# State kept zero-padded, and output products run together with the next chunk's state update

## The chip, the cores and the metric

The kernel runs on one core of one Trainium2 chip. Times are device microseconds (us) of one execution. The profile shows the engines of that core: PE (TensorE, matrix products; its weight loads are listed apart, as PEld), DVE (VectorE), ACT (ScalarE), POOL (GpSimd) and SP (SyncE, which here only starts transfers).

## The reference

Two parts follow each other. The first is linear attention with a state of its own for each of 4 batches and 8 heads (768 tokens, head width 48, all float32):

```
for t in range(S):
    cur = einsum('bhd,bhe->bhde', u * kt, vt)
    y[:, :, t] = einsum('bhd,bhde->bhe', rt, state + cur)
    state = wt[:, :, :, None] * state + einsum('bhd,bhe->bhde', kt, vt)
```

The second is a feed-forward block over the 3072 tokens (width 384, hidden width 2048): `h = x @ w_in`, `g = h * sigmoid(1.702 h)`, `out = g @ w_out`.

## The kernel before, in words

**The feed-forward part.** Tokens are taken in six groups of 512 (`CHUNKS`, four chunks of 128 each), the hidden width in 16 slices of 128. One task is a group and a slice. A task has a first product (token `g`, lines 346 to 348: nine matmuls of 128x128 weights with 512 columns), the gelu (token `h`, lines 357 to 359: two passes on ACT, one on DVE) and a second product (token `y`, lines 372 to 374: nine matmuls). Each product is made of three, from high and low halves of the numbers. `y` runs two tasks behind `g` (`LAG`). There are 106 tasks; group 0 is cut finer at its start.

**The attention part.** There are 24 chunks of 128 tokens, six to a batch. A chunk needs the state that the chunk before it left; a batch's first chunk has none, and its last leaves none. The eight heads are four pairs: a pair's two heads lie on partitions 0 to 47 and 64 to 111 (`head(h)`). `chunk(t)` is a generator of twelve pieces, which the text counts from 0:

- pieces 0 to 2 (DVE): two scans of the decays, products with k and r, which give `kf` and `qf` (lines 224 to 246);
- piece 3: `ps_d` matmuls (line 252), in chunks 0 to 7 only;
- piece 4 (DVE): diagonal sums `s`, and the old state times the chunk's total decay, in place (line 262);
- piece 5: `kf` transposed on PE (line 268) and copied to `kt` by ACT (line 270);
- piece 6 (ACT): eight diagonal matrices `am` (line 277);
- piece 7: the state update: `ps_u` = `kt` times `v` (lines 284 and 285, 16 matmul records), added to the decayed state by DVE (line 290; ACT copies it where there is no old state, line 288);
- piece 8: score matmuls `ps_s` (line 296); piece 9: they are copied into `am` by a mask (DVE, line 299);
- piece 10: the outputs, `ps_y`: `am` times `v` (line 309, 16 matmul records), then, on the same accumulators, the state product, old state times `qf` (line 316, 16 matmul records);
- piece 11: `ps_y` is split into high and low halves of the feed-forward input `x` (ACT line 194, DVE line 195).

A float32 product appears in the records as two matmuls, so 16 records are 8 products: four pairs, two heads. Line 309 and the state update use all 128 partitions as rows and 64 or 48 columns of the array. Line 316 uses 48 rows and 48 columns: head 0's state is at rows and columns 0 to 47, head 1's at 64 to 111.

All small PSUM tiles share three buffers (`psa`). `kt`, `lp` and each of the two `am` tiles have one buffer, `kq` and the state two.

**Order of the work.** It is written out by hand. The first part is the list `RAMP`, up to task 41, which also loads and converts the weights (tokens `f` and `w`: 12 conversions on ACT and DVE, lines 180 to 190). From task 42 (`FIRST`) on, `rest()` makes the order from `PARTS`: a list of pieces with the step at which each comes, counted from the chunk's begin, either ahead of the task's `g` (0) or behind it (1). Tokens `l` load a chunk, `m` measures it (ACT, line 200), `x` starts the DMAs (line 334) that fill the gaps of `x`. In this order, every four tasks, one chunk puts four groups of small matmuls between the big ones, each behind another `g`: `ps_t`, then `ps_u`, then `ps_s`, then `ps_y`.

Of the kernel before, what the change touches and what calls it, by code (L numbers as in the profile page):

```python
# [8 lines left out]
F32 = mybir.dt.float32  # L9
# [4 lines left out]
AF = mybir.ActivationFunctionType  # L14
# [38 lines left out]
TASKS += [(0, 2, 4, f) for f in range(5, 10)] + [(0, 0, 4, f) for f in range(10, NF)]  # L53
TASKS += [(i, 0, n, f) for i, n in enumerate(CHUNKS) if i for f in range(NF)]

PARTS = [("a", 0, 0), ("a", 1, 0), ("a", 2, 0), ("m", 2, 0), ("a", 2, 1), ("a", 3, 0), ("m", 3, 0), ("l", 3, 0),
         ("l", 3, 0), ("a", 3, 1), ("a", 4, 0), ("a", 4, 1), ("a", 5, 1), ("a", 5, 1), ("a", 6, 1), ("a", 6, 1), ("x", 6, 1)]
BEFORE = 9

# [14 lines left out]
y38 a13 y39 h40 x11 g41 h41 m12  # L76
"""
WIDE = 512
PAD = 528
assert sum(CHUNKS) == NT  # L80


# [1 line left out]
def rwkv_ffn_kernel(ctx: ExitStack, tc, wkr, vp, vrk, ub, w_in, w_out, masks, vt, uc, out):  # L84
# [41 lines left out]
    acc = cp.tile([P, 2 * NT + 2 * NL], F32, name="acc")  # L126
    G.memset(acc, 0.0)
    wih, wil, woh, wol = (cp.tile([P, NF, DM], F32R, name=x) for x in ("wih", "wil", "woh", "wol"))

    loaded, state, pools = {}, {}, {}  # L130

# [79 lines left out]
    def chunk(t):  # L211

        i, col = where[t]
        a, v = loaded[t][:2]
        n, nc_ = NP * CW, NP * C
        w0, w1 = a[:, 0:n], a[:, 1 : n + 1]
        k = a[:, n + 1 : n + 1 + nc_].rearrange("r (p c) -> r p c", p=NP)
        r = a[:, n + 1 + nc_ :].rearrange("r (p c) -> r p c", p=NP)
        first, final = t % CB == 0, (t + 1) % CB == 0

        lp = at.tile([R2, 2 * n], F32, tag="lp", name="lp")
        li, pm = (lp[:, i * n : (i + 1) * n].rearrange("r (p c) -> r p c", p=NP) for i in range(2))
        total = li[:, :, 0:1]
        V.tensor_tensor_scan(  # L224
            li.rearrange("r p c -> r (p c)")[:, ::-1], w1[:, ::-1],
            d1r.rearrange("r p c -> r (p c)")[:, ::-1], 0.0, op0=ALU.mult, op1=ALU.add,
        )
        V.reciprocal(d1f[:, :, 0:1], total)
        yield
        V.tensor_tensor_scan(  # L230
            pm.rearrange("r p c -> r (p c)"), w0,
            d1f.rearrange("r p c -> r (p c)"), 0.0, op0=ALU.mult, op1=ALU.add,
        )
        s = at.tile([P, H], F32, tag="s", name="s", bufs=2)
        if t < WHOLE:
            rk = at.tile([R2, NP, C], F32, tag="rku", name="rku")
            V.tensor_tensor(rk, r, k, op=ALU.mult)
        else:
            rt, kt_ = loaded[t][2][:, 0:DM], loaded[t][2][:, DM:]
            V.tensor_tensor(rt, rt, kt_, op=ALU.mult)  # L240
        yield

        kq = at.tile([R2, 2 * nc_], F32, tag="kq", name="kq", bufs=2)
        kf, qf = (kq[:, i * nc_ : (i + 1) * nc_].rearrange("r (p c) -> r p c", p=NP) for i in range(2))
        V.tensor_tensor(kf, k, li[:, :, 1:CW], op=ALU.mult)
        V.tensor_tensor(qf, r, pm[:, :, 0:C], op=ALU.mult)
        measures[t] = measured(t, lp, kq)
        yield
        if t < WHOLE:
            ps_d = ps_a.tile([P, NP, 2], F32, tag="psa", name="ps_d")  # L250
            for p in range(NP):
                T.matmul(ps_d[:, p], rk[:, p], u_heads[:, p], start=True, stop=True)  # L252
        yield
        if t < WHOLE:
            V.tensor_copy(s, ps_d.rearrange("p n h -> p (n h)"))
        else:
            V.tensor_tensor(rt, rt, u_sb, op=ALU.mult)
            V.tensor_reduce(s, rt.rearrange("p (h d) -> p h d", d=D), axis=AX.X, op=ALU.add)
        sf = None
        if not first:  # L260
            sf = state[t - 1]
            V.tensor_tensor(sf, sf, total.broadcast_to([R2, NP, D]), op=ALU.mult)
        loaded.pop(t)
        yield
        if not final:
            ps_t = ps_a.tile([P, NP, R2], F32, tag="psa", name="ps_t")
            for p in range(NP):
                T.transpose(ps_t[:, p], kf[:, p], ident[0:R2, 0:R2])  # L268
            kt = at.tile([P, NP, R2], F32, tag="t", name="kt")
            A.copy(kt, ps_t)  # L270
        yield
        am = []
        for h in range(2):
            x_ = at.tile([P, NP, C], F32, tag=f"am{h}", name="am")
            am.append(x_)
            for p in range(NP):
                A.activation(x_[:, p], ident, AF.Copy, scale=s[:, 2 * p + h : 2 * p + h + 1])  # L277
        yield

        if not final:  # L280
            ps_u = ps_a.tile([R2, NP, D], F32, tag="psa", name="ps_u")
            for p in range(NP):

                T.matmul(ps_u[0:HB, p], kt[:, p, 0:HB], v[:, 2 * p], start=True, stop=True)  # L284
                T.matmul(ps_u[HB:R2, p], kt[:, p, HB:R2], v[:, 2 * p + 1], start=True, stop=True)  # L285
            new = state[t] = at.tile([R2, NP, D], F32, tag="sf", name="sf", bufs=2)
            if sf is None:
                A.copy(new, ps_u)
            else:
                V.tensor_tensor(new, ps_u, sf, op=ALU.add)  # L290
        yield

        ps = [ps_a.tile([P, NP, C], F32, tag="psa", name=f"ps_s{h}") for h in range(2)]
        for p in range(NP):
            for h in range(2):
                T.matmul(ps[h][:, p], kf[head(h), p], qf[head(h), p], start=True, stop=True)  # L296
        yield
        for h in range(2):
            V.copy_predicated(am[h], after_b, ps[h])  # L299
        yield  # L300
        cs = slice(col * C, (col + 1) * C)
        ps = ps_a.tile([R2, NP, C], F32, tag="psa", name="ps_y")
        v_ = v.rearrange("p h d -> p (h d)")

        for p in range(NP):
            for h in range(2):
                at_, m = ((0, HB), (HB, D))[h]
                c = (2 * p + h) * D
                T.matmul(  # L309
                    ps[at_ : at_ + m, p], v_[:, c : c + m], am[h][:, p],  # L310
                    start=p == 0, stop=sf is None and p == NP - 1, skip_group_check=True,
                )
        if sf is not None:
            for p in range(NP):
                for h in range(2):
                    T.matmul(  # L316
                        ps[head(h), p], sf[head(h), p], qf[head(h), p],
                        start=False, stop=p == NP - 1, skip_group_check=True,
                    )
        yield  # L320
        if i not in xs:
            xs[i] = new_x(i)
        x = xs[i]
        split(x[0:R2, 0, :, cs], x[0:R2, 1, :, cs], ps)
        state.pop(t - 1, None)
        yield
# [8 lines left out]
                    x[dst : dst + 16, :, m, c0:c1].bitcast(F32), x[j : j + 16, :, NM, c0:c1].bitcast(F32)  # L335
                )

    xs, po, parts, measures = {}, {}, {}, {}

    def first_product(j, task):  # L340
        i, c0, c1, f = task
# [46 lines left out]
    with tc.manual_schedule():  # L388
# [17 lines left out]
        def do(token):  # L406
# [18 lines left out]
            elif kind == "u":  # L425
                nc.sync.dma_start(u_sb, ub)
            elif kind == "M":
                A.dma_start(hm[0:D], masks[0:D])
                A.dma_start(hm[HB:R2], masks[D:R])
            elif kind == "g":  # L430
                first_product(i, TASKS[i])
            elif kind == "h":
                gelu(i, TASKS[i])
            elif kind == "y":
                second_product(i, TASKS[i])
                group = TASKS[i][0]
                if i == last[group]:
                    store(group, starts[group] * C, CHUNKS[group] * C)

        def rest():  # L440

            begins = []
            for t, (i, col) in enumerate(where):
                n = len([x for x in TASKS if x[0] == i - 1])
                begins.append(last.get(i - 1, -1) + 1 - BEFORE - round((CHUNKS[i] - 1 - col) * n / CHUNKS[i]))
            ramp = dict(told)
            for j in range(FIRST, len(TASKS) + LAG):
                for post in range(2):
                    if post and j < len(TASKS):
                        yield f"g{j}"  # L450
                        yield f"h{j}"
                    for t, begin in enumerate(begins):
                        for kind, step, half in PARTS:
                            token = f"{kind}{t + 2 * (kind == 'l')}"
                            if (step + begin, half) > (j, post) or kind == "l" and t + 2 >= NT:
                                continue
                            if ramp.get(token, 0):
                                ramp[token] -= 1
                            elif (step + begin, half) == (j, post):
                                yield token  # L460
                if j - LAG >= 0 and f"y{j - LAG}" not in told:
                    yield f"y{j - LAG}"

        for token in RAMP.split():
            do(token)
        for token in rest():
            do(token)

# [116 lines left out]
```

## Time and profile before

| What | Value |
|---|---|
| Time, median of 3 runs | 549.38 us (547.93 to 551.22) |
| The profiled execution | 545.92 us, of which 544.3 us lie between its first and last instruction |
| Granted TensorE clock, mean | 0.994 of full |
| PE busy | 521.7 us (96%), 3462 matmul records |
| DVE busy, ACT busy | 282.4 us (52%), 284.0 us (52%) |

A row of the page's groups has a line, an engine and operation, the tile written and those read, shapes, the count, then the busy time in us and the mean time of one in ns, then the idle time ahead of them on that engine. A row of the timeline has the start in us, the time from the first start to the last end of the instructions merged in it, the engine and line, and the count. Matmuls overlap in the array, so that what a matmul costs is the distance to the next one's start and not its own length.

### The profile page before, as it was taken

To read this page: it belongs to the slowest core of one execution; us is meant where nothing else is said; L and a number is where in the kernel's file an instruction comes from. 1 tells how busy PE (TensorE), PEld (TensorE's weight loads), DVE (VectorE), ACT (ScalarE), POOL (GpSimd) and SP (SyncE) were. 2 spreads that over 40 slices of the span, in tenths; PEclk is the share of its full clock that TensorE was granted. 3 is DMA by queue.
4 is the path that set the end of the run, shared out by engine and by line. 5 is a ranking of instruction groups with operands and counts; after the bars stand their busy time and mean duration, and the time that the engine had idled before them with its cause. 6 is when DMAs were issued, how large, how long until landed. Compare 5 with 4: busy or idle time off the path is not lost.

```text
span 544.3 us, 8703 instructions
## 1 busy us (share of the span) xinstructions
PE 521.7 (96%) x3462; PEld 431.8 (79%) x3462; DVE 282.4 (52%) x438; ACT 284.0 (52%) x616; POOL 32.4 (6%) x69
## 2 busy tenths in 40 slices
PE   2898999999999999999999999999999999999994
PEld 1788999888878788787777787788788787888883
DVE  4798798977635563553544554545445423112110
ACT  2888868976635545655354364454364442322221
POOL 3110200000100001000001000001000001000000
PEclk9999999999999999999999999999999999999998
DMA  8989899243623432234313244213240001010001
GB/s 190 212 170 220 194 225 230 58 97 95 182 51 95 96 97 70 67 88 94 66 30 91 56 131 94 54 43 83 63 133 1 0 1 31 21 39 0 1 0 64
DMA packets 17506, 48.10 MB, mean 88 GB/s; under 512 B 3024, under 2 KB 6416, under 8 KB 17456
## 3 DMA queue, kind: packets, MB, share of 16 engines
q1 hardware_dynamic: 14096, 36.02, 26.0%
q0 software_dynamic: 3104, 11.13, 10.1%
q8 instruction: 29, 0.48, 0.4%
q10 hardware_dynamic: 256, 0.30, 0.2%
q14 instruction: 21, 0.17, 0.1%
HBM read 40.36 MB, written 4.72 MB: 83 GB/s over the span
## 4 chain that ended last, share of the span: by engine, by line
PE 89%; DMA 2%; DVE 1%; ACT 1%; SPq 0%; issue 0%
PE po L372 14%; PE ph L346 12%; PE po L374 12%; PE po L373 12%; PE ph L348 12%; PE ph L347 12%; PE ps_s L296 4%; PE ps_y L309 4%; PE ps_y L316 3%; DMA st<-in_w_out 2%; PE ps_u L284 1%; PE ps_t L268 1%; PE ps_d L252 1%; PE ps_u L285 1%; SPq L334 0%; DVE st L183 0%
## 5 line engine op out<-in xcount | busy, mean ns | idle before, releaser
L359 DVE TENSOR_TENSOR gl<-gf,gh 128x512 fp32r<-128x512 f32 (+1 forms) x106 | 67.6, 639 | 204.9 <-ACT gf L358 201.6
L357 ACT ACTIVATE gh<-ph 128x512 fp32r<-128x512 f32 (+1 forms) x106 | 59.0, 557 | 184.6 <-PE ph L348 176.4
L372 PE MATMUL po<-gh,woh 128*128 128x512 f32 (+1 forms) x318 | 123.5, 388 | 0.0
L346 PE MATMUL ph<-x,wih 128*128 128x512 f32 (+1 forms) x318 | 120.3, 378 | 0.0
L348 PE MATMUL ph<-x,wil 128*128 128x512 f32 (+1 forms) x318 | 118.7, 373 | 1.4 <-DVE wil L190 1.4
L347 PE MATMUL ph<-x,wih 128*128 128x512 f32 (+1 forms) x318 | 118.6, 373 | 0.0
L374 PE MATMUL po<-gl,woh 128*128 128x512 f32 (+1 forms) x318 | 118.4, 372 | 0.0
L373 PE MATMUL po<-gh,wol 128*128 128x512 f32 (+1 forms) x318 | 118.3, 372 | 0.0
L372 PEld LDWEIGHTS po<-gh,woh 128*128 128x128 f32 x318 | 60.7, 191 | 13.6 <-issue 2.6
L348 PEld LDWEIGHTS ph<-x,wil 128*128 128x128 f32 x318 | 61.1, 192 | 11.8 <-DVE wil L190 1.6
L346 PEld LDWEIGHTS ph<-x,wih 128*128 128x128 f32 x318 | 61.1, 192 | 11.2 <-issue 1.0
L374 PEld LDWEIGHTS po<-gl,woh 128*128 128x128 f32 x318 | 60.6, 191 | 10.6 <-DVE gl L359 0.3
L347 PEld LDWEIGHTS ph<-x,wih 128*128 128x128 f32 x318 | 61.2, 192 | 9.7
L373 PEld LDWEIGHTS po<-gh,wol 128*128 128x128 f32 x318 | 60.7, 191 | 8.6
L277 ACT ACTIVATE am<-ident,s 128x128 f32<-128x128 f32 x192 | 58.8, 398 | 7.3 <-PE ps_y L309 5.7
L358 ACT ACTIVATE gf<-ph 128x512 f32<-128x512 f32 (+1 forms) x106 | 58.7, 553 | 0.0
L299 DVE COPY_PREDICATED am<-after,ps_s 128x512 f32<-128x512 int32 x48 | 32.6, 729 | 5.9 <-ACT am L277 3.3
L224 DVE TENSOR_TENSOR_SCAN lp<-wkr_t,d1r 112x516 f32<-112x516 f32 x24 | 29.5, 1229 | 6.2 <-POOL d1r L102 4.2
L296 PE MATMUL ps_s<-kq 48*128 48x128 f32 x384 | 31.8, 304 | 0.0
L296 PEld LDWEIGHTS ps_s<-kq 48*128 48x128 f32 x384 | 26.6, 204 | 5.8 <-issue 4.6
L309 PE MATMUL ps_y<-am,v_t 128*64 128x128 f32 (+1 forms) x384 | 29.2, 291 | 0.5 <-DVE am L299 0.5
L230 DVE TENSOR_TENSOR_SCAN lp<-wkr_t,d1f 112x516 f32<-112x516 f32 x24 | 29.4, 1224 | 0.1
(62 smaller groups left out, 473.9 us busy)
## 6 DMA issues: line engine op xcount, KB each, us to landing
wkr_t<-in_wkr SPq DMA_DIRECT2D x23, 385.2 KB, 5.0
wkr_t<-in_wkr POOLq DMA_DIRECT2D x23, 288.9 KB, 5.5
st<-in_w_out SPq DMA_DIRECT2D x6, 1024.0 KB, 10.4
rk_t<-in_vrk SPq DMA_DIRECT2D x16, 384.0 KB, 4.5
v_t<-in_vrk SPq DMA_DIRECT2D x24, 192.0 KB, 4.5
out_t<-ob SPq DMA_DIRECT2D x18, 256.0 KB, 2.0
st<-in_w_in POOLq DMA_DIRECT2D x6, 384.0 KB, 9.6
st<-in_w_in SPq DMA_DIRECT2D x6, 384.0 KB, 11.4
```

The lines of the kernel that those rows point to most:

```text
L277: A.activation(x_[:, p], ident, AF.Copy, scale=s[:, 2 * p + h : 2 * p + h + 1])
L296: T.matmul(ps[h][:, p], kf[head(h), p], qf[head(h), p], start=True, stop=True)
L309: T.matmul(ps[at_ : at_ + m, p], v_[:, c : c + m], am[h][:, p], start=p == 0, stop=sf is None and p == NP - 1, skip_group_check=True,)
L346: T.matmul(ph, h_, xs[i][:, 0, c, cs], start=c == 0, stop=False)
L347: T.matmul(ph, h_, xs[i][:, 1, c, cs], start=False, stop=False)
L348: T.matmul(ph, l_, xs[i][:, 0, c, cs], start=False, stop=c == NM - 1)
L357: A.activation(gh, ph, AF.Gelu_apprx_sigmoid, scale=1.0 / W_SCALE)
L358: A.activation(gf, ph, AF.Gelu_apprx_sigmoid, scale=1.0 / W_SCALE)
L359: V.tensor_tensor(gl, gf, gh.bitcast(F32), op=ALU.subtract)
L372: T.matmul(o, woh[:, f, ms], gh, start=first, stop=False, skip_group_check=True)
L373: T.matmul(o, wol[:, f, ms], gh, start=False, stop=False, skip_group_check=True)
L374: T.matmul(o, woh[:, f, ms], gl, start=False, stop=f == NF - 1, skip_group_check=True)
```

## The change

Each chunk's state is kept in a tile of twice the width: a pair's two heads have a column block each, and the rows that belong to the other head hold zeros. Two such tiles are filled with zeros by POOL in the ramp, and the chunks take them in turn. So the state product of line 316 takes all 112 partitions as rows (with `qf` of both heads as the moving data) and 48 columns, that is, the array's rows are no longer divided there. The decay multiplies the wide tile; the add of the state update, and the copy where there is no old state, is done once for each head. The state update takes 48 columns for both heads.

From task 42 on (`steady`), pieces 6 and 7 change places: the update comes first and the diagonals second. `PARTS` puts the outputs of a chunk (its last two pieces) and the update and diagonals of the next chunk behind the same task's `g`, the outputs first; `BEFORE` goes from 9 to 11, so that a chunk begins two tasks earlier, and its last two pieces stay behind the same task as before. Pieces of chunks 12 and 13 whose place in the new order lies ahead of task 42 are put at its start, half a step apart. In the ramp the order is as it was. The list `tiled` is never filled, so its branch is not run, and the extra `x` tokens for chunks that don't end a group do nothing. The spare tile `PAD` shrinks by what the state tiles grow.

```diff
-PARTS = [..., ("m", 3, 0), ("l", 3, 0),
-         ("l", 3, 0), ("a", 3, 1), ("a", 4, 0), ("a", 4, 1), ("a", 5, 1), ("a", 5, 1), ("a", 6, 1), ("a", 6, 1), ("x", 6, 1)]
-BEFORE = 9
+PARTS = [..., ("m", 3, 0), ("a", 3, 1), ("a", 4, 1),
+         ("a", 4, 1), ("l", 5, 0), ("l", 5, 0), ("a", 5, 1), ("a", 5, 1), ("a", 8, 1), ("a", 8, 1), ("x", 8, 1)]
+BEFORE = 11
...
-PAD = 528
+PAD = 144
...
+    states = [at.tile([R2, NP, 2, D], F32, tag=f"sf{i}", name="sf") for i in range(2)]
...
-            V.tensor_tensor(sf, sf, total.broadcast_to([R2, NP, D]), op=ALU.mult)
+            flat = sf.rearrange("r p h d -> r p (h d)")
+            V.tensor_tensor(flat, flat, total.broadcast_to([R2, NP, R]), op=ALU.mult)
...
+        def update():
...
             for p in range(NP):
-                T.matmul(ps_u[0:HB, p], kt[:, p, 0:HB], v[:, 2 * p], start=True, stop=True)
-                T.matmul(ps_u[HB:R2, p], kt[:, p, HB:R2], v[:, 2 * p + 1], start=True, stop=True)
-            new = state[t] = at.tile([R2, NP, D], F32, tag="sf", name="sf", bufs=2)
-            if sf is None:
-                A.copy(new, ps_u)
-            else:
-                V.tensor_tensor(new, ps_u, sf, op=ALU.add)
+                for h in range(2):
+                    T.matmul(ps_u[head(h), p], kt[:, p, head(h)], v[:, 2 * p + h], start=True, stop=True)
+            new = state[t] = states[t % 2]
+            for h in range(2):
+                if sf is None:
+                    A.copy(new[head(h), :, h], ps_u[head(h)])
+                else:
+                    V.tensor_tensor(new[head(h), :, h], ps_u[head(h)], sf[head(h), :, h], op=ALU.add)
+        for part in (update, diagonal) if steady else (diagonal, update):
+            part()
+            yield
...
                     T.matmul(
-                        ps[head(h), p], sf[head(h), p], qf[head(h), p],
+                        ps[head(h), p], sf[:, p, h], qf[:, p],
                         start=False, stop=p == NP - 1, skip_group_check=True,
                     )
...
+                for sf in states:
+                    G.memset(sf, 0.0)
```

More of the change, by code (lines that the diff above doesn't have):

```diff
@@ L54 @@
 TASKS += [(i, 0, n, f) for i, n in enumerate(CHUNKS) if i for f in range(NF)]
-PARTS = [("a", 0, 0), ("a", 1, 0), ("a", 2, 0), ("m", 2, 0), ("a", 2, 1), ("a", 3, 0), ("m", 3, 0), ("l", 3, 0),
-         ("l", 3, 0), ("a", 3, 1), ("a", 4, 0), ("a", 4, 1), ("a", 5, 1), ("a", 5, 1), ("a", 6, 1), ("a", 6, 1), ("x", 6, 1)]
-BEFORE = 9
+PARTS = [("a", 0, 0), ("a", 1, 0), ("a", 2, 0), ("m", 2, 0), ("a", 2, 1), ("a", 3, 0), ("m", 3, 0), ("a", 3, 1), ("a", 4, 1),
+         ("a", 4, 1), ("l", 5, 0), ("l", 5, 0), ("a", 5, 1), ("a", 5, 1), ("a", 8, 1), ("a", 8, 1), ("x", 8, 1)]
+BEFORE = 11
 FIRST = 42
@@ L265, in chunk @@
         if not final:
-            ps_t = ps_a.tile([P, NP, R2], F32, tag="psa", name="ps_t")
-            for p in range(NP):
-                T.transpose(ps_t[:, p], kf[:, p], ident[0:R2, 0:R2])
             kt = at.tile([P, NP, R2], F32, tag="t", name="kt")
-            A.copy(kt, ps_t)
-        yield
[L272 to L277, printed above, removed]
@@ L278, in chunk @@
-        yield
-        if not final:
+            if tiled:
+                ps = [ps_a.tile([P, NP, D], F32, tag="psa", name=f"ps_t{h}") for h in range(2)]
+                for p in range(NP):
+                    for h in range(2):
+                        T.transpose(ps[h][:, p], kf[head(h), p], ident[head(h), head(h)])
+                for h in range(2):
+                    A.copy(kt[:, :, head(h)], ps[h])
+            else:
+                ps_t = ps_a.tile([P, NP, R2], F32, tag="psa", name="ps_t")
+                for p in range(NP):
+                    T.transpose(ps_t[:, p], kf[:, p], ident[0:R2, 0:R2])
+                A.copy(kt, ps_t)
@@ L281, in chunk, with diagonal @@
+        yield
+        am, sums = [], []
+        def diagonal():
+            for h in range(2):
+                x_ = at.tile([P, NP, C], F32, tag=f"am{h}", name="am")
+                am.append(x_)
+                for p in range(NP):
+                    A.activation(x_[:, p], ident, AF.Copy, scale=s[:, 2 * p + h : 2 * p + h + 1])
+        def update():
+            if final:
+                return
             ps_u = ps_a.tile([R2, NP, D], F32, tag="psa", name="ps_u")
             for p in range(NP):
-                T.matmul(ps_u[0:HB, p], kt[:, p, 0:HB], v[:, 2 * p], start=True, stop=True)
@@ L285, in chunk @@
-                T.matmul(ps_u[HB:R2, p], kt[:, p, HB:R2], v[:, 2 * p + 1], start=True, stop=True)
-            new = state[t] = at.tile([R2, NP, D], F32, tag="sf", name="sf", bufs=2)
-            if sf is None:
-                A.copy(new, ps_u)
-            else:
-                V.tensor_tensor(new, ps_u, sf, op=ALU.add)
-        yield
+                for h in range(2):
+                    T.matmul(ps_u[head(h), p], kt[:, p, head(h)], v[:, 2 * p + h], start=True, stop=True)
+            new = state[t] = states[t % 2]
@@ L293, in chunk @@
+            for h in range(2):
+                if sf is None:
+                    A.copy(new[head(h), :, h], ps_u[head(h)])
+                else:
+                    V.tensor_tensor(new[head(h), :, h], ps_u[head(h)], sf[head(h), :, h], op=ALU.add)
+        for part in (update, diagonal) if steady else (diagonal, update):
+            part()
+            yield
         ps = [ps_a.tile([P, NP, C], F32, tag="psa", name=f"ps_s{h}") for h in range(2)]
@@ L336, in fill_x @@
                 )
-    xs, po, parts, measures = {}, {}, {}, {}
+    xs, po, parts, measures, tiled, steady = {}, {}, {}, {}, [], []
     def first_product(j, task):
@@ L445, in rest @@
                 begins.append(last.get(i - 1, -1) + 1 - BEFORE - round((CHUNKS[i] - 1 - col) * n / CHUNKS[i]))
-            ramp = dict(told)
+            done, plan = dict(told), {}
+            for t, begin in enumerate(begins):
+                late = 0
+                for kind, step, half in PARTS:
+                    token = f"{kind}{t + 2 * (kind == 'l')}"
+                    if done.get(token, 0):
+                        done[token] -= 1
+                    elif kind != "l" or t + 2 < NT:
+                        at_ = 2 * (step + begin) + half
+                        if at_ < 2 * FIRST:
+                            at_ = 2 * FIRST + late
+                            late += 1
+                        plan.setdefault(at_, []).append(token)
             for j in range(FIRST, len(TASKS) + LAG):
@@ L451, in rest @@
                         yield f"h{j}"
[L452 to L460, printed above, removed]
+                    yield from plan.get(2 * j + post, ())
                 if j - LAG >= 0 and f"y{j - LAG}" not in told:
@@ L465, in rwkv_ffn_kernel @@
             do(token)
+        steady.append(True)
         for token in rest():
```

## Prediction

> **What bounds the kernel now.** I read the page first, then the waits of PE, then the timeline of PE around one chunk. From the page:
>
> ```profile
> PE 521.7 (96%) x3462; PEld 431.8 (79%) x3462; DVE 282.4 (52%) x438; ACT 284.0 (52%) x616; POOL 32.4 (6%) x69
> ...
> PE   2898999999999999999999999999999999999994
> ...
> PE 89%; DMA 2%; DVE 1%; ACT 1%; SPq 0%; issue 0%
> ```
>
> PE is busy in all but the first slices, and 89% of the chain that ended last is PE. Among the waits of PE the last one in time that is worth naming is this, and the chain of waits shows what it waited for:
>
> ```profile
> PE ph L348 <- DVE wil L190: 1.4, 1, 1.4
> ```
> ```profile
> 49.30 0.26 DVE sf L262
> 49.57 1.15 DVE wil L190
> ```
>
> So up to 50.7 us the ramp is bound by transfers, ACT and DVE, and an edit there is worth what it does to DVE. Behind that PE never stops, and each microsecond taken out of PE's sequence is a microsecond of the span, as long as no other engine becomes late. What small matmuls cost PE is read from distances between starts. One chunk's outputs and state product, from the timeline of PE:
>
> ```profile
> 329.21 0.39 PE L348 MATMUL ph<-x,wil 128*128 128x512 f32 x1
> 329.53 1.09 PE L309 MATMUL ps_y<-am,v_t 128*64 128x128 f32 x16
> 330.55 1.08 PE L316 MATMUL ps_y<-kq,sf 48*48 48x128 f32 x16
> 331.55 0.50 PE L372 MATMUL po<-gh,woh 128*128 128x512 f32 x1
> 331.89 0.39 PE L373 MATMUL po<-gh,wol 128*128 128x512 f32 x1
> ```
>
> and a stretch of the ramp in which a state update happens to follow an output run directly:
>
> ```profile
> 124.77 0.39 PE L346 MATMUL ph<-x,wih 128*128 128x512 f32 x1
> 125.00 0.39 PE L347 MATMUL ph<-x,wih 128*128 128x512 f32 x1
> 125.22 0.39 PE L348 MATMUL ph<-x,wil 128*128 128x512 f32 x1
> 125.45 0.55 PE L268 MATMUL ps_t<-ident,kq 112*128 112x112 f32 x4
> 125.93 1.09 PE L309 MATMUL ps_y<-am,v_t 128*64 128x128 f32 x16
> ...
> 127.40 0.50 PE L372 MATMUL po<-gh,woh 128*128 128x512 f32 x1
> 127.73 0.40 PE L373 MATMUL po<-gh,wol 128*128 128x512 f32 x1
> ```
>
> Big matmuls start 0.225 us apart (125.22 less 124.77, halved). The run at 329 costs 331.89 - 329.21 - 2 x 0.225 = 2.23 us. Within it the length of one matmul gives the stride (columns: least, median, greatest length in ns):
>
> ```profile
> L309 PE MATMUL ps_y<-am,v_t x384: 272/273/476, 20.8 to 455.2; 128*48 128x128 f32 x168, 128*64 128x128 f32 x24
> ```
>
> The 16 records of line 309 last 1.09 us, the last of them 0.273, so they start (1.09 - 0.273)/15 = 0.054 us apart, the last at 330.35. Line 316 begins 0.20 us later, at 330.55: at the place where the array goes from whole columns to quadrants the distance is 0.20 instead of 0.054.
>
> **State products in whole-row tiles.** Line 316 keeps its 16 records, each with 128 columns streamed. In the new shape they stand on line 309's division of the array (all rows, 48 of 64 columns), so I price them at line 309's stride, and the step between the lines at the same 0.054. That saves 0.20 - 0.054 = 0.15 us a chunk. From below: nothing is saved, if the 0.20 comes from something else than the division. From above: 0.15 is all that there is. I take 0.15, since the merged stretch of the ramp (next part) shows that a change of tile and operands without a change of division is cheap. 20 of the 24 chunks have a state product, 10 of them (13 to 17, 19 to 23) behind the ramp.
>
> The Trainium skill, in "TensorEngine Tiling (Array Packing)", Key Properties, says that different tiles can load and multiply in parallel; by that the old quadrants, two of which are used in turn, would run two heads at once, and the change would give that up, at an estimate of half of 16 x 0.054 us a chunk, 8.6 us over 20 chunks. The trace disagrees: 16 records in quadrants take 1.08 us, 16 that fill all rows take 1.09.
>
> **Update and outputs in one run.** Before, the update stands alone:
>
> ```profile
> 340.03 0.39 PE L348 MATMUL ph<-x,wil 128*128 128x512 f32 x1
> ...
> 341.28 0.39 PE L373 MATMUL po<-gh,wol 128*128 128x512 f32 x1
> ```
>
> It costs 341.28 - 340.03 - 0.45 = 0.80 us. In the ramp stretch above, line 309's last start is 125.93 + 0.82 = 126.75, and the next big matmul comes at 127.40, 0.65 later. With no update between, that distance is 331.55 - (330.55 + 0.81) = 0.19. So the update costs 0.46 us inside a run: saved are 0.34 us. Behind the ramp the updates of chunks 14, 15, 16 and 18 to 22 join a run of the chunk before (chunks 17 and 23 have none): 8 x 0.34 = 2.7 us. From above it would be nine with chunk 13's, from below zero, if the joined update had to wait. It needs `kt`, which ACT copies a whole task earlier; its PSUM buffer comes from the previous chunk's scores, masked three tasks earlier. Neither is near. What is now queued on ACT behind the output's cast is the eight diagonals, a task ahead of the masking that needs them, and then the group's stores; PE has over 4 us of big products meanwhile. If that cover were gone, masking would wait, and with it only `ps_y` three tasks later.
>
> **The seam at task 42.** Here the new order puts chunk 12's outputs, chunk 13's transposes, its `kt` copy and its update behind one `g`. The copy cannot be early: ACT runs gelu, the cast, then the copy. These are ACT's rows at that place, and the copy's mean:
>
> ```profile
> 226.38 0.60 ACT L357 ACTIVATE gh<-ph 128x512 fp32r<-128x512 f32 x1 [3.23 <-PE ph L348]
> 226.88 0.59 ACT L358 ACTIVATE gf<-ph 128x512 f32<-128x512 f32 x1
> 227.42 0.59 ACT L194 CAST x<-ps_y 112x512 fp32r<-112x512 f32 x1
> ```
> ```profile
> L270 ACT COPY kt<-ps_t 128x448 f32<-128x448 f32 x20 | 10.7, 536 | 29.2 <-PE ps_t L268 29.2
> ```
>
> The copy would end near 227.42 + 0.59 + 0.54 = 228.55. PE gets there earlier. Its row for the same outputs:
>
> ```profile
> 226.28 1.09 PE L309 MATMUL ps_y<-am,v_t 128*64 128x128 f32 x16
> ```
>
> The last of them starts at 227.10, then 0.20 for the change and the four transposes (0.48 from their start to the next line's, 125.45 to 125.93): 227.8. PE waits 0.75 us, once, and everything behind it on PE with it. Two more changes of division in that run cost about 0.2, and joining saves 0.34: together +0.6 us. Chunk 13's second scan and products move ahead of task 42 on DVE; they need only what the ramp has loaded, and DVE is half idle there, so I cost this at nothing.
>
> **Added work on DVE, ACT and POOL.** From the groups by line:
>
> ```profile
> L240 DVE TENSOR_TENSOR rk_t<-rk_t 128x384 f32<-128x384 f32 x16 | 8.5, 532 | 0.0
> ...
> L262 DVE TENSOR_TENSOR sf<-sf,lp 112x192 f32<-112x192 f32 x20 | 7.0, 348 | 0.0
> ...
> L290 DVE TENSOR_TENSOR sf<-ps_u,sf 112x192 f32<-112x192 f32 x16 | 5.6, 349 | 4.9 <-PE ps_u L285 4.9
> ```
>
> The wide decay is priced as line 240, which has its 384 elements: +0.18 us, 20 times. The add becomes two of half the partitions; I take each at the full 0.35, so +0.35, 16 times (from below +0). The page's 52% for DVE is an average over stages; for the tight one I take a row of the windows (stretch, its length, then busy time and count of PE, PEld, DVE, ACT and POOL):
>
> ```profile
> 50.70:114.00 63.30, 63.24 (x544) 59.72 (x545) 56.88 (x81) 52.33 (x110) 6.17 (x13) 0.97 0.74 163
> ```
>
> DVE is 90% busy between 50.7 and 114 us, and there two places matter. First, chunk 3's decay lies on the chain at 49.30 just ahead of the `wil` on which PE waits: +0.18, and about 0.1 from chunk 1's doubled add earlier, while chunk 3's state product gives back 0.15. Second, the transposes of chunk 6 at 113.86 follow closely on their operand:
>
> ```profile
> 112.73 0.68 DVE L246 TENSOR_TENSOR kq<-wkr_t,lp 112x512 f32<-112x512 f32 x1
> ```
> ```profile
> 113.86 0.58 PE L268 MATMUL ps_t<-ident,kq 112*128 112x112 f32 x4
> ```
>
> The slack is 113.86 - 113.41 = 0.45; DVE is late by one doubled add and one wide decay, 0.53. So chunk 4's gain is lost there and 0.08 more. Up to 114 us that makes about +0.2. Behind it chunks 5 and 7 to 11 gain 6 x 0.15 = 0.9. POOL's two fills come in the first microseconds, ahead of two weight transfers, and hide in what ACT and DVE then wait for other things.
>
> **The sum.** 10 x 0.15 = 1.5 and 2.7 and 0.9 saved, 0.6 and 0.2 paid: -4.3 us. Against the profiled execution, 545.92 us (544.3 between its instructions), this is 541.6. That execution is 3.5 us below the median of the runs shown; the forecast for the median is 549.38 - 4.3 = 545.1. A change of 0.5%, 2.75 us, is about what a measurement of this kernel can tell from no change.
>
> **Rivals.** (a) *The 0.20 us step stays*, because it belongs to the change from one line's operands to the next and not to the division. Against it: at 126.75 the same kind of step cost at most 0.46 with all 16 records of the update. Then 1.5 + 0.9 are not saved and chunk 3's 0.15 too: about -1.8, 547.6.
>
> (b) *DVE bounds more of the ramp than I read.* All that it gets up to 114 us (five wide decays, four doubled adds, 0.9 + 1.4 = 2.3) reaches PE instead of 0.2: -2.2, 547.2. For it speaks the 90%; against it that DVE idles for ACT and transfers several times within the stretch.
>
> (c) *With all rows taken, the weight load no longer hides.* Both heads' tiles now use the same rows, where quadrants used different ones. The loads last:
>
> ```profile
> L309 PEld LDWEIGHTS ps_y<-am,v_t 128*64 128x64 f32 (+1 forms) x384 | 22.4, 136 | 8.0 <-issue 5.4 <-DVE am L299 1.1 <-DVE kq L245 0.4
> L316 PEld LDWEIGHTS ps_y<-kq,sf 48*48 48x48 f32 x320 | 17.1, 123 | 3.7 <-issue 3.6
> ```
>
> If each of the 320 loads stood in series with the matmul before it, 320 x 0.123 = 39 us would be added: 584. It decides from 4.3/320 = 13 ns per record on (no gain left), and is a loss that can be measured from 22 ns. Against it: line 309's loads last 136 ns on whole rows, and its matmuls still start 54 ns apart. The Trainium skill, in "TensorE: Matmul & The Clock Gate", Part 3, states that a load overlaps running matmuls only where the row group differs; by that rule line 309 would already run at over 136 ns a record, and the trace disagrees.
>
> (d) *The joined update waits in every run* as it does at the seam: 8 x 0.75 = 6 us, +1.7, 551.1. For it I find no queue; it stands for what I overlook.
>
> **Chances.** Forecast 0.70, (a) 0.10, (b) 0.10, (c) 0.04, (d) 0.06. The likeliest case gives 545.1, in it from 543.3 (all 20 products and nine updates gain: -6.1) to 547. Runs of the old kernel lie 1.5 to 1.8 us off their median, so the lower end is 541.8; the upper, which takes in (a) and (b) with that scatter, is 549.2. Faster by over 0.5%: 0.66 (nearly all of the forecast, a little of (a) and (b)); within 0.5%: 0.27; slower: 0.07, (c) and half of (d).
>
> **What would show it.** In the changed profile line 316 should have the shape 112*48 and start 0.05 after line 309's last; a run with outputs, state product and update should cost 2.23 - 0.15 + 0.46 = 2.54 us instead of 2.23 + 0.80; one wait of `ps_u` on `kt` of 0.75 us near task 43, and only one; no new wait of PE on DVE but about 0.1 at chunk 6's transposes. Strides above 60 ns in line 316 would make it (c), a step of 0.20 between the lines (a), and waits of `ps_u` in each run (d).

## The result and the profile after

The changed kernel takes 542.80 us in the median of 4 runs (541.80 to 543.58), against 549.29 us (547.93 to 551.22, 4 runs) before: a ratio of 0.9878, with a 95% interval of 0.9844 to 0.9913. That is 6.5 us less, where 4.3 were forecast. The profiled execution took 543.58 us, 542.0 of them between its instructions, at a granted clock of 0.982.

From the page of the changed kernel, its engines, PE's slices and the summary of the chain:

```profile
PE 512.2 (95%) x3462; PEld 428.9 (79%) x3462; DVE 294.4 (54%) x454; ACT 284.5 (52%) x620; POOL 32.8 (6%) x71
...
PE   1788899999999999999999999999999999999994
...
PE 86%; ACT 3%; DMA 3%; SPq 1%; DVE 1%; issue 0%; ACTq 0%
```

PE has the same 3462 records and is busy 9.5 us less. DVE has 12.0 us more. The chain is still mostly PE, so the question is again where PE's starts lie.

The profile that came with the changed kernel is only 2.3 us below the one of before (543.58 and 545.92), though the medians are 6.5 apart. Two rows show why. The first is the start of the 25th task's first product, just behind the ramp, the second that of the 106th and last. From the timeline of PE before:

```profile
116.40 0.50 PE L346 MATMUL ph<-x,wih 128*128 128x512 f32 x1
...
527.94 0.39 PE L346 MATMUL ph<-x,wih 128*128 128x512 f32 x1
```

and after:

```profile
120.06 0.50 PE L366 MATMUL ph<-x,wih 128*128 128x512 f32 x1
...
526.00 0.39 PE L366 MATMUL ph<-x,wih 128*128 128x512 f32 x1
```

Between them lie 411.54 us before and 405.94 after: 5.60 us saved in PE's sequence. Up to the first of them the changed kernel is 3.66 us later. The experiments show that this start moves by 2 to 3 us between executions whose work up to there is the same. Two things make it late in this profile: PE waits 2.35 us at 67.35 for a transfer that fills `x`, and from 68.6 to 72.0 us the granted clock is 0.50, where big matmuls of 256 columns start 0.21 us apart instead of 0.12. From the 9th to the 11th first product that costs 1.3 us. Between the 25th and the 106th the granted clock is 1.00 in every profile of this study, so the clock has no part in the 5.60.

What became of one chunk's run, now with the next chunk's update in it, stands in the timeline of PE after:

```profile
370.94 0.39 PE L368 MATMUL ph<-x,wil 128*128 128x512 f32 x1
371.26 1.09 PE L329 MATMUL ps_y<-am,v_t 128*64 128x128 f32 x16
372.18 1.04 PE L336 MATMUL ps_y<-kq,sf 112*48 112x128 f32 x16
373.05 0.53 PE L301 MATMUL ps_u<-v_t,kt 128*48 128x48 f32 x16
373.51 0.50 PE L392 MATMUL po<-gh,woh 128*128 128x512 f32 x1
373.85 0.40 PE L393 MATMUL po<-gh,wol 128*128 128x512 f32 x1
```

By the prediction's rule the run costs 373.85 - 370.94 - 0.45 = 2.46 us, where 2.23 + 0.80 = 3.03 were paid before and 2.54 were forecast. The last record of line 329 starts at 371.26 + 1.09 - 0.27 = 372.08, and line 336 begins 0.10 later; before, that step was 0.20.

The timeline merges the 16 records of a line. Taken singly from the trace, they start two by two: one record for head 0's half of the columns and one for head 1's, 0.007 us apart, and the next two 0.109 later. Before, the quadrants of line 316 do the same. So 0.054 is a mean that no two records keep, and a step of 0.10 between two lines is no more than the distance within a line: at the entry to the state product nothing extra is left. Before, two things were extra there: 0.10 at the entry, and 0.03 behind the first two records of line 316 (0.147 to the next two, against 0.113 in line 336).

At the seam (behind the first product of task 43, with tasks counted from 0 as in the code), from the same view:

```profile
228.42 0.39 PE L368 MATMUL ph<-x,wil 128*128 128x512 f32 x1
228.74 1.09 PE L329 MATMUL ps_y<-am,v_t 128*64 128x128 f32 x16
229.76 0.60 PE L280 MATMUL ps_t<-ident,kq 112*128 112x112 f32 x4
230.98 0.56 PE L301 MATMUL ps_u<-v_t,kt 128*48 128x48 f32 x16 [0.62 <-ACT kt L281]
231.48 0.50 PE L392 MATMUL po<-gh,woh 128*128 128x512 f32 x1
231.81 0.39 PE L393 MATMUL po<-gh,wol 128*128 128x512 f32 x1
```

The forecast wait of `ps_u` on `kt` is there. The bracket counts 0.62 us from the end of the last transpose; by the prediction's working, from where the update could have started, it is 230.98 - 229.76 - 0.48 = 0.74. The run costs 2.94 us. Its three parts stood apart before, at 1.22, 0.41 and 0.80, so the seam costs 0.51 us net. Behind the 25th first product it is the only wait of PE on another engine.

The groups by line of the changed kernel show the state product, its loads, the add and the decay:

```profile
L336 PE MATMUL ps_y<-kq,sf 112*48 112x128 f32 x320 | 22.2, 281 | 0.0
L336 PEld LDWEIGHTS ps_y<-kq,sf 112*48 112x48 f32 x320 | 19.4, 129 | 0.0
...
L307 DVE TENSOR_TENSOR sf<-ps_u,sf 48x192 f32<-48x192 f32 x32 | 11.2, 350 | 4.4 <-PE ps_u L301 4.2
L265 DVE TENSOR_TENSOR sf<-sf,lp 112x384 f32<-112x384 f32 x20 | 11.0, 548 | 0.0
```

The doubled add takes 350 ns each time, and the wide decay 548 instead of 348: +0.35 and +0.20 a chunk, as forecast (+0.35 and +0.18). The loads of line 336 last 129 ns instead of 123, and its 16 records start (1.04 - 0.27)/15 = 0.051 us apart on average.

### The profile page after: what moved, and what is told of

It is laid out like the page before. It is cut to its first block, busy times and chain, and to the rows that moved or that the text cites. A ratio compares the mean times of both kernels' runs of the same rounds, so it can differ in the third digit from the quotient of the medians.

```text
span 542.0 us, 8721 instructions
## 1 busy us (share of the span) xinstructions
PE 512.2 (95%) x3462; PEld 428.9 (79%) x3462; DVE 294.4 (54%) x454; ACT 284.5 (52%) x620; POOL 32.8 (6%) x71
## 4 chain that ended last, share of the span: by engine, by line
PE 86%; ACT 3%; DMA 3%; SPq 1%; DVE 1%; issue 0%; ACTq 0%
PE po L392 13%; PE ph L366 12%; PE po L394 12%; PE po L393 12%; PE ph L368 12%; PE ph L367 12%; PE ps_s L316 4%; PE ps_y L329 4%; PE ps_y L336 3%; DMA st<-in_w_out 2%; PE ps_u L301 1%; PE ps_t L280 1%; DMA x<-x 1%; PE ps_d L254 1%; SPq L354 1%; ACT am L291 0%
## 5 line engine op out<-in xcount | busy, mean ns | idle before, releaser
L368 PE MATMUL ph<-x,wil 128*128 128x512 f32 (+1 forms) x318 | 118.5, 372 | 1.3 <-DVE wil L192 1.3
L394 PE MATMUL po<-gl,woh 128*128 128x512 f32 (+1 forms) x318 | 118.4, 372 | 0.0
L329 PEld LDWEIGHTS ps_y<-am,v_t 128*64 128x64 f32 (+1 forms) x384 | 22.9, 139 | 9.1 <-issue 5.5
```

The costliest lines, as they stand in the source:

```text
L329: T.matmul(ps[at_ : at_ + m, p], v_[:, c : c + m], am[h][:, p], start=p == 0, stop=sf is None and p == NP - 1, skip_group_check=True,)
L368: T.matmul(ph, l_, xs[i][:, 0, c, cs], start=False, stop=c == NM - 1)
L394: T.matmul(o, woh[:, f, ms], gl, start=False, stop=f == NF - 1, skip_group_check=True)
```

## The experiments

Three theories were to be told apart. *The division*: what is saved is the array's change from whole rows to quadrants and back, and a run that keeps one division is cheap throughout. *The order*: the joining alone saves, and the wide state little. *The halves*: the old quadrants ran two heads at once, and the new shape should have lost something that another term hides. All times of before beside them are runs on the same chip.

**The wide state alone, in the order of before** (of the diff only `states`, the zero fills, the wide decay, the add by heads, and this):

```diff
-                        ps[head(h), p], sf[head(h), p], qf[head(h), p],
+                        ps[head(h), p], sf[:, p, h], qf[:, p],
```

> The wide state in the order of before; the update keeps its 64 and 48 columns. Theory (a change of the array's division costs PE about 0.1 us more than a step without one): the run of outputs and state product costs 2.09 us as in the changed kernel, instead of 2.23, the update alone stays at 0.80; 17 of 20 state products lie where PE never waits, 17 x 0.14 = 2.4 us saved, less up to 0.2 paid by VectorE in the ramp: about -2.2 us. Rival 1 (the whole gain comes from joining the update, the wide state only makes that possible): run unchanged at 2.23, no difference. Rival 2 (the wider VectorE work in the ramp is paid in full, 2.3 us): about 0.

It took 546.34 us (12 runs) against 548.64 (23 runs), ratio 0.9960 (0.9941 to 0.9980): 2.3 us less. From its timeline of PE:

```profile
370.92 0.39 PE L352 MATMUL ph<-x,wil 128*128 128x512 f32 x1
371.24 1.09 PE L313 MATMUL ps_y<-am,v_t 128*64 128x128 f32 x16
372.16 1.05 PE L320 MATMUL ps_y<-kq,sf 112*48 112x128 f32 x16
373.13 0.50 PE L376 MATMUL po<-gh,woh 128*128 128x512 f32 x1
373.47 0.40 PE L377 MATMUL po<-gh,wol 128*128 128x512 f32 x1
```

The run costs 2.10 us instead of 2.23, with the step at 0.10 here too. From the 25th to the 106th first product it saves 1.9 us: 15 state products lie there, 0.13 each. So the 0.10 that is gone belonged to the division and not to the change of operands. The 0.10 that stays is the distance within a line.

**The new order alone, with the narrow state** (all of the diff but the wide state; the update keeps 64 and 48 columns).

> The new order with the narrow state in quadrants; the update keeps its 64 and 48 columns. Theory: the joined run has two changes of division inside (columns to quadrants to columns) and costs about 2.78 us against 2.23 + 0.80 = 3.03 apart, so 0.25 saved in seven runs and 0.34 in the one without a state product, 2.1 us, less 0.5 at the seam: about -1.6 us, clearly less than what is left when the -2.2 of the wide state alone is taken from the change's -6. Rival 1 (what is saved is the entry and the exit of the run, the divisions inside do not matter): joined run about 2.45 as in the changed kernel, about -4 us in all.

547.64 us (12 runs), ratio 0.9983 (0.9964 to 1.0001): 1.0 us less, not surely different from no change, but its sequence of PE between the two first products is 1.2 us shorter. Its joined run, from the timeline of PE:

```profile
372.04 0.39 PE L364 MATMUL ph<-x,wil 128*128 128x512 f32 x1
372.36 1.09 PE L325 MATMUL ps_y<-am,v_t 128*64 128x128 f32 x16
373.38 1.08 PE L332 MATMUL ps_y<-kq,sf 48*48 48x128 f32 x16
374.39 0.26 PE L297 MATMUL ps_u<-v_t,kt 128*64 128x48 f32 x1
...
374.98 0.50 PE L388 MATMUL po<-gh,woh 128*128 128x512 f32 x1
375.32 0.40 PE L389 MATMUL po<-gh,wol 128*128 128x512 f32 x1
```

2.83 us: behind quadrants the update costs 0.60, of the 0.80 that it costs alone. The two steps of 0.20 (into the quadrants and out of them) can both be seen. The two parts of the change therefore don't add: 1.9 and 1.2 us in PE's sequence apart, 5.6 together. Neither part alone has the narrower update, which a run below prices.

**The kernel before, profiled once more.** No edit; what is asked is where two executions of one kernel differ.

> The kernel before, once more, for its ramp. The profiled execution of before took 545.92 us, the timed ones 547.93 to 551.22; behind the ramp the matmuls of the trace repeat to 0.01 us. Theory: the difference lies in the ramp up to about 75 us (transfers of x and the weights) and nowhere else: here the 11th first product begins later than the 72.8 us of the profile shown, by as much as the execution is longer than 545.92. Rival: it lies in the long part, as slightly longer strides.

547.45 us, 1.5 more than the profile of before. The 25th first product starts at 118.37 instead of 116.40, and from there to the 106th it takes 411.51 us (411.54). The ramp is 1.97 us longer (1.08 at the 11th first product, where the expectation looked), and what stands behind the start of the 106th is 0.41 shorter. Over all profiles of this study the 25th first product starts between 116.2 and 120.1 us: at 116.4 and 118.4 for the kernel before, at 120.1 and 119.5 for the changed one, but at 116.9 and 118.5 for the mended seam below, whose work up to there is the changed kernel's. Between the two first products, two executions of a kernel agree to 0.03 us, so that a single profile tells of PE's sequence to some hundredths, and of the ramp only to some 4 us.

**The changed kernel with 64 columns for head 0's update**, as before:

```diff
-                for h in range(2):
-                    T.matmul(ps_u[head(h), p], kt[:, p, head(h)], v[:, 2 * p + h], start=True, stop=True)
+                T.matmul(ps_u[0:HB, p], kt[:, p, 0:HB], v[:, 2 * p], start=True, stop=True)
+                T.matmul(ps_u[HB:R2, p], kt[:, p, HB:R2], v[:, 2 * p + 1], start=True, stop=True)
```

> The changed kernel with 64 columns again for head 0 in the state update (48 for head 1), all else as changed. Theory: the update's cost depends on its columns: 0.80 instead of 0.70 alone, 0.46 instead of 0.36 in a joined run, so a joined run costs 2.55 instead of 2.45 and 1.6 us are lost over 16 updates behind 72 us. Rival (the shorter update comes from its new place or from the padded state): joined run stays at 2.45.

Its joined run, in the timeline of PE:

```profile
370.37 0.39 PE L368 MATMUL ph<-x,wil 128*128 128x512 f32 x1
...
373.03 0.50 PE L392 MATMUL po<-gh,woh 128*128 128x512 f32 x1
373.37 0.40 PE L393 MATMUL po<-gh,wol 128*128 128x512 f32 x1
```

2.55 us instead of 2.46, and 407.42 us from the 25th to the 106th first product instead of 405.94. The 16 columns fewer are worth 0.10 us in each of 15 updates, 1.5 us in all. So the new shape and the new order together, without the narrower update, save 411.54 - 407.42 = 4.1 us, against 1.9 + 1.2 apart. A single execution took 543.46 us; its quicker ramp (118.33) hides the loss.

**The changed kernel, timed again.** No edit.

> The changed kernel once more, timed beside before on the same chip. Theory: behind 116 us the profiles of before and after differ by 5.6 us in PE's sequence alone, and the ramp differs only by its scatter: 5.6 us less than before, ratio 0.990, within 1 us. Rival (the change also makes the ramp faster, which the first timing's 6.5 us would allow): 6.5 us or more, and the 25th first product ahead of 117 us in most profiles of the wide state.

543.42 us (6 runs) against 548.24 (12 runs), ratio 0.9908 (0.9879 to 0.9938): 4.8 us less, and 405.95 us between the two first products.

**The seam mended.** The transposes of chunk 13 go ahead of the first product of task 43 instead of behind it; the update stays behind chunk 12's outputs:

```diff
-                            at_ = 2 * FIRST + late
+                            at_ = 2 * FIRST + min(late, 2)
```

> The changed kernel with chunk 13's transposes put ahead of the first product of task 43 instead of behind it. Theory: the 0.88 us between its transposes and its update go, as ScalarE copies during that product; outputs and update form one run of 1.57 us and the transposes cost 0.41 alone, 1.98 instead of 2.94, so 0.96 us less from there on. Rival (the copy is late for another reason, such as ScalarE's backlog): the wait stays.

The run at the seam, from the timeline of PE:

```profile
225.64 0.39 PE L368 MATMUL ph<-x,wil 128*128 128x512 f32 x1
225.95 1.09 PE L329 MATMUL ps_y<-am,v_t 128*64 128x128 f32 x16
226.87 0.53 PE L301 MATMUL ps_u<-v_t,kt 128*48 128x48 f32 x16
227.33 0.50 PE L392 MATMUL po<-gh,woh 128*128 128x512 f32 x1
227.66 0.39 PE L393 MATMUL po<-gh,wol 128*128 128x512 f32 x1
```

1.57 us without a wait, and 0.41 for the transposes where they now stand: 1.98 instead of 2.94. A single execution took 539.64 us; 1 us of what it is below the changed kernel comes from the seam, the rest from an early 25th first product (116.87).

**Both heads' states in one tile of 112 columns**, the zeros filling the other blocks: 8 records of the whole array instead of 16 of half its columns, put ahead of the outputs.

```diff
+        if sf is not None:
+            for p in range(NP):
+                T.matmul(ps[:, p], sf[:, p], qf[:, p], start=p == 0, stop=False, skip_group_check=True)
```

> The changed kernel with the two heads' states as one block-diagonal 112 x 112 tile, so that the state product takes 8 matmul records (112 rows, 112 columns) instead of 16, ahead of the outputs and in the division of the big products. It tells what sets the distance between small matmuls. Theory 1 (the weight load sets it, by its columns: transposes with 112 columns start about 0.10 apart, updates with 64 and 48 columns 0.027, with 48 only 0.024): 8 records about 0.095 apart, a joined run of about 2.35 us instead of 2.45. Theory 2 (the streamed columns set it, 128 in 0.054): 8 records 0.054 apart, a joined run of about 2.05 us.

```profile
246.74 1.04 PE L326 MATMUL ps_y<-kq,sf 112*112 112x128 f32 x8
247.71 1.09 PE L331 MATMUL ps_y<-am,v_t 128*64 128x128 f32 x16
248.62 0.53 PE L300 MATMUL ps_u<-v_t,kt 128*48 128x48 f32 x16
```

In these rows of its timeline of PE, 8 records start (1.04 - 0.27)/7 = 0.11 us apart. Half the records at twice the distance make the same run, 2.46 us, and neither theory had that number. A single execution took 540.74 us, with the 25th first product at 116.24. That early ramp hides a sequence of PE that is 0.95 us longer than the changed kernel's (406.89); 0.69 of it is one wait of a first product on ACT at 207.91.

**Scores in the same manner**, on top of the mended seam: GpSimd copies `qf` into a zero-padded tile `qp`, and one product with 256 columns streamed takes both heads of a pair.

```diff
+                G.tensor_copy(qp[0][head(h), :, h], qf[head(h)])
...
+                T.matmul(o, kf[:, p], qp[0][:, p], start=True, stop=True)
```

> The seam mended as in the run before, and behind the ramp the scores without a change of division too: GpSimd copies qf into a tile with zeros in the other head's rows, and each pair's scores are one product of 112 rows, 128 columns of weights and 256 streamed columns, 8 records instead of 16. Theory: 8 records 0.107 apart (256 streamed columns, which hide a load of 128) and no change at either end: 0.87 us a run instead of 1.29, 11 runs, 4.6 us less, and 0.96 from the seam: 5.6 us below the changed kernel, about 0.979 of before. Rival (GpSimd's copies are too slow, or slow VectorE down, so that masks and outputs come late): PE waits at the scores or the outputs and nothing or less is gained.

551.55 us (7 runs), ratio 1.0067 (1.0042 to 1.0093): slower. From its timeline of PE:

```profile
255.82 0.40 PE L380 MATMUL ph<-x,wil 128*128 128x512 f32 x1
256.06 1.89 PE L325 MATMUL ps_s<-qp,kq 112*128 112x256 f32 x8
257.60 0.58 PE L404 MATMUL po<-gh,woh 128*128 128x512 f32 x1
258.02 0.40 PE L405 MATMUL po<-gh,wol 128*128 128x512 f32 x1
```

Records with 256 columns start 0.216 us apart, twice 0.11, and the run costs 258.02 - 255.82 - 0.45 = 1.75 us instead of 1.30. My expectation of this run was wrong by that factor of two. 11 such runs make 5 us. PE's sequence, 9.1 us longer than with the mended seam alone, loses some 4 us more: the last task lasts 4.16 us from one first product to the next instead of 4.08, with no small matmul in it. Why the big matmuls are further apart there is open.

**The two heads' outputs one after the other**, in the changed kernel (line 329), so that records no longer alternate between the two halves of the columns:

```diff
-        for p in range(NP):
-            for h in range(2):
+        for h in range(2):
+            for p in range(NP):
```

> The changed kernel with the output products in another order: all four pairs of head 0, then all of head 1, instead of the two heads in turn. Same instructions. Theory (a float32 record streams a column in about 0.84 ns, so 128 in 0.108 us, as the run with 256 columns in 0.216 shows; the 0.054 between records comes from two column halves of the array that work side by side when their records alternate): records of one head queue behind each other, about 0.11 apart, and the 16 take about 1.7 us instead of 0.87; a run of outputs, state product and update costs about 3.2 us instead of 2.45. Rival (0.054 is the rate of any record with 64 columns or fewer of weights, by its weight load): unchanged at 2.45.

At the seam, where line 336 is left out of the run, the timeline of PE has

```profile
231.01 1.57 PE L329 MATMUL ps_y<-am,v_t 128*64 128x128 f32 x16
```

16 records take 1.57 - 0.27 = 1.30 us from the first start to the last, instead of 0.82. In runs with a state product the first records of head 0's state start among the last ones of head 1's outputs:

```profile
253.47 0.31 PE L336 MATMUL ps_y<-kq,sf 112*48 112x128 f32 x1
253.58 0.27 PE L329 MATMUL ps_y<-am,v_t 128*48 128x128 f32 x1
253.62 0.27 PE L336 MATMUL ps_y<-kq,sf 112*48 112x128 f32 x1
253.69 0.27 PE L329 MATMUL ps_y<-am,v_t 128*48 128x128 f32 x1
```

Each half keeps its own distance of 0.11 us and does not wait for the other. Such a run costs 2.94 us, less than if the lines stood behind each other. The expected 1.7 and 3.2 us were too high: all 16 records were taken to queue, but in the trace head 1's first record starts beside the fifth of head 0. A single execution took 551.97 us.

**The same swap in the kernel before** (line 316, the quadrants):

> The kernel before with the state products in quadrants in another order: head 0's four, then head 1's four. Same instructions. Theory (the two diagonal quadrants also worked side by side, which is why the padded tiles, two column halves, are no slower and no faster than they): about 0.11 between records, a run of outputs and state product of about 3.0 us instead of 2.23. Rival (the forecast's reading, that the quadrants were not used in parallel): unchanged at 2.23.

```profile
251.02 0.39 PE L348 MATMUL ph<-x,wil 128*128 128x512 f32 x1
251.34 1.09 PE L309 MATMUL ps_y<-am,v_t 128*64 128x128 f32 x16
252.35 1.55 PE L316 MATMUL ps_y<-kq,sf 48*48 48x128 f32 x16
253.83 0.50 PE L372 MATMUL po<-gh,woh 128*128 128x512 f32 x1
254.17 0.39 PE L373 MATMUL po<-gh,wol 128*128 128x512 f32 x1
```

1.55 - 0.27 = 1.28 us for the 16 records instead of 0.81, and 2.70 for the run instead of 2.23 (about 3.0 were expected, for the same reason too much); a single execution took 555.43 us. 15 such runs lie between the two first products, which are 418.61 us apart instead of 411.54. Quadrants and column halves behave alike: alternating records run side by side in two tiles, and records of one tile follow each other 0.11 us apart.

**The mended seam, timed.**

> The changed kernel with the seam mended, timed. From the trace 0.96 us less than the changed kernel, which lies 5.6 us under before: 6.6 us under before, ratio 0.988, if its single look (539.64 us) owed the rest to a quick ramp; 0.984 or less if it did not.

541.10 us (4 runs, 539.73 to 541.78) against 548.65 (7 runs), ratio 0.9854 (0.9829 to 0.9879): 7.6 us less between the medians, 8.0 by the ratio. The trace accounts for 6.6 of it, at the very edge of the interval. The other 1.0 to 1.4 us I can't place; it is no more than the ramp moves. This is the fastest version.

## Why the prediction was right, and where it was off

**PE's sequence bounds the kernel**: right. Against 6.5 us in the first timing and 4.8 in the second, 5.6 are found as distances between starts of PE. The terms of the sum that lie there made 4.35 in the forecast: 15 state products at 0.15, eight joined updates at 0.34, less 0.6 for the seam. They measured like this:

| Term, behind the 25th first product | forecast us | measured us |
|---|---|---|
| state products | 15 x 0.15 = 2.25 | 15 x 0.135 = 2.0 |
| updates joined | 8 x 0.34 = 2.7 | 8 x 0.44 = 3.5 |
| updates of the ramp, 48 columns for 64 | 0 | 6 x 0.10 = 0.6 |
| the one update of the ramp that already followed a state product | 0 | 0.15 |
| seam | -0.6 | -0.5 |
| the small product `ps_n` at the end, no longer in an output run | 0 | 0.15 |
| the big matmuls, over some 1400 distances | 0 | -0.3 |
| sum | 4.35 | 5.6 (5.60 in the trace) |

The last but one row has no known cause; the wide state alone shows the same 0.3.

**State products.** "I price them at line 309's stride, and the step between the lines at the same 0.054." The mechanism was right, and the size came out right in part by luck. The price took a mean for a step: single records start 0.007 or 0.109 us apart, the step fell to 0.10 and not to 0.054, and the other 0.03 came from behind line 316's first two records. Rival (a), that the 0.20 stays, is refuted by the wide state alone. Rival (c) is refuted by loads of 129 ns where each half of the columns starts a record every 109.

**The joined update: the term that was mis-sized.** "The update costs 0.46 us inside a run" holds for the update as it stood in the quoted stretch, with 64 and 48 columns: with 64 columns put back the joined run costs 2.55, 0.45 above the 2.10 of outputs and state product. The prediction left out that the diff also cuts head 0's update to 48 columns, which it read and didn't price. That is 0.10 us in each update, joined or not, 1.5 us in all and thus more than the sum is off.

**Why the two parts don't add.** Narrow state and new order pay 0.60 for the update behind quadrants; with whole rows ahead of it the same update costs 0.45. That makes 7 x 0.15 = 1.0 us, since the eighth joined run is of outputs and update alone and costs 1.67 us behind the narrow state and with 64 columns put back alike. With the 1.5 us of columns it is 2.5, the 2.5 us that lie between 1.9 + 1.2 and 5.6. So of the three theories the division holds, with the narrower update beside it; the order alone explains 1.2 us.

**The seam.** The wait was forecast at 0.75 and is 0.74; the net cost at 0.6 and is 0.5. Its place and its cause were right, and an order that moves the transposes half a step takes it away. No other run waits, so rival (d) falls.

**The ramp.** DVE's additions have the forecast sizes, but their price of 0.2 us can't be seen where starts move by 4 us. PE's new waits in the first 70 us (2.35 us on the transfer that fills `x`, in the changed kernel's profile) come and go between executions: that wait stands in both profiles of the changed kernel and in the one of the wide state alone (1.9 to 2.5 us), but neither in the two of the mended seam nor in the one with 64 columns, and in none of the four with the narrow state. The half clock behind it stands in the two of the changed kernel alone. So a price of the wide state in the ramp of up to 1 us stays open; so does a small form of rival (b), while its full 2.2 us don't agree with the timings, which give 6.5 and 4.8 where PE's sequence saves 5.6, 2.3 for 1.9 and 7.6 for 6.6. The wait at chunk 6's transposes was not seen.

**The tiles that work side by side: wrong, without harm to the sum.** The prediction set aside the rule of the Trainium skill ("TensorEngine Tiling (Array Packing)", Key Properties) that tiles load and multiply in parallel, since 16 records took 1.08 us in quadrants and 1.09 on whole rows. The comparison was of two cases that both run in parallel. Two heads' records start 0.007 us apart in both; once records don't alternate, both take 1.28 to 1.30 instead of 0.81, so the page is right for the quadrants of before as for the column halves of after, and the change gave up nothing because the halves of the columns serve as well as the quadrants did. The estimate of 8.6 us lost, 0.43 a chunk, had the right rule and nearly the right price (0.47 with the quadrants by head); it missed that line 309 lives by the rule too. The other rule ("TensorE: Matmul & The Clock Gate", Part 3: a load overlaps only where the row group differs) finds no support in these runs: both heads' loads of 129 ns use the same rows, and each half of the columns starts a record every 109 ns.

## What to carry to other kernels

Price a run of small matmuls by starts, and count the changes of the array's division in it: here each costs about 0.1 us more than a change of operands, so that putting work of one division together, padded with zeros if need be, is worth more than the two steps apart (4.1 us against 1.9 + 1.2). Two tiles ran at once throughout only where neighbouring records alternated between them; read it off single starts, or by comparing with an order that doesn't alternate, not by comparing two shapes that both do. Price every edit of a diff, a slice that gets narrower too, and compare profiles from a mark behind the start-up if that varies from one execution to the next.

## What the runs showed of the hardware

- A record of a float32 product streams 128 columns in about 0.11 us and 256 in 0.216 on the whole array. Products of half the columns in alternation start two by two, 0.007 apart and then 0.109, so one whole-array product in place of two halves saves nothing (a run of 2.46 us both ways).
- Fewer weight columns shorten a short product: with 48 columns streamed, 16 records with 48 weight columns take 0.10 us less than with 64 and 48 in turn.
- Records of different column halves need not wait for each other: with the outputs in order of heads, head 0's next line starts among head 1's records.
- The first 116 to 120 us, with weights and inputs loading, differ by up to 3.8 us over the profiles here, by 2.0 and 3.2 where the work up to there is the same, and the 406 to 412 us behind them by 0.03 for one kernel. A half of the granted clock for 3.4 us, behind a wait of PE, is part of it in two of them.
